# The first four chunks by halves, one stretch for Y, D and G, and a new order

## The chip, the core and the metric

The kernel runs on one core of a Trainium2 chip. The core has TensorE (PE, matmuls; its weight loads are listed as PEld), VectorE (DVE), ScalarE (ACT), GpSimd (POOL) and the DMA queues, of which this kernel uses those of SyncE (SP) and ScalarE. The metric is device time in microseconds. The kernel before takes 120.8 us (median of 3 runs, 120.77 to 120.96).

## The reference

Two parts run one after the other. The first is a Mamba-2 style scan over 4 sequences of 768 positions with 8 heads, in chunks; the second is a feed-forward layer with GELU.

```python
# first part, per sequence and head, chunk after chunk
cum   = cumsum(log(clip(a, 1e-6, 1)))
M     = (C @ B.T) * exp(cum_i - cum_j) * (i >= j)
y     = M @ x + (C @ state) * exp(cum_i)
state = exp(cum_last) * state + sum_j exp(cum_last - cum_j) * outer(B_j, x_j)
# second part, on all 3072 tokens of 256 values
h   = y_tokens @ w_in               # 256 -> 2048
out = gelu_tanh(h) @ w_out          # 2048 -> 256
```

The result does not depend on the chunk length; the kernel uses chunks of 128 positions instead of 32.

## The kernel before

A sequence has 6 chunks of 128, so there are 24 chunks, worked in 12 pairs u = 0 to 11. Instead of exp and log the kernel takes products of the clipped decays, by a scan that runs backwards through a chunk (lines 325 to 329). B is multiplied by these products and C by their reciprocals, so that the Gram product of both already holds the decay.

Each pair goes through these steps. G is the Gram matmul of scaled B and C (line 574, tiles of 32x128). M masks it with a triangle (line 584). D makes each chunk's addition to the state (line 607, tiles of 128x32), S updates the state and SP spreads it into blocks (lines 655 and 662). Y is the output of the scan, from the state (line 629) and from M (line 638), both in tiles of 128x32; yev moves it from PSUM to SBUF. Then s1 is the first feed-forward matmul in eight steps of four (line 688), gelu takes each of them on ACT (line 692), and s2 is the second feed-forward matmul: for each of the two chunks four groups of four (line 706), then oev copies the result out and store writes it.

Sequence 0 is prepared in its own way, because nothing can start before it. Its first four chunks (pairs 0 and 1) come with four loads aq.0 to aq.3 of the decays, one for each chunk of all sequences, one load each of B and C (load_bc0, line 147) and one of x (load_x4, line 180). With four consecutive positions in a partition, chunk 0 is in partitions 0 to 31, chunk 1 in 32 to 63, and so on. clipq, Rq (the scan), tpq (a transpose) and recip0 make the factors; mulb and mulc (lines 413 and 406) scale B and C; mulc keeps even and odd heads apart, with zeros between. tw transposes them on TensorE (line 422) and ew copies the result to SBUF. x4 casts x, XX brings it into the right order and XD makes D for pairs 0 and 1 (lines 542 and 552). The mask of pair 0 is split: M.0.0 on DVE, and GE (ACT) with ME (POOL, line 595) for the rest. Chunks 4 and 5 come with bc1 and mul1, T1, ce1, bh1, N1, bn1. The other sequences come with one load each of B and C, with mul, T, E, F, N and bn.

The weights are loaded in four quarters each (load_wi, load_wo) and cast in halves (wi.q.k, wo.q.k). The first s1 of a pair needs the cast quarter 0 of w_in and yev of the pair.

The order of all work is written out by hand in the string ORDERED. Each engine takes its steps from it in that order and in no other; an ending such as :A, :D or :P says which engine runs a step that can run on several. The loads and stores stand in SP's queue in the same order (or ACT's, with :A). `~n` puts n units of filler on TensorE, matmuls with zeros of 128 columns a unit (line 676); `name+n` puts them in front of an s1 step.

PSUM is narrow: two banks "hp" are shared by s1, D, XX, tw and pp, one bank "o" by s2 and some of the first transposes, two pairs "ga" and "gb" by G and transposes, and one bank "yb" by Y and the last s2.

Of the kernel before, what the change touches and what calls it, by code (L numbers as in the profile page):

```python
# [29 lines left out]
mul.1.0 s1.1.7 load_x.3 Y.2 yev.2.0.2 s2.0.1.1.o wo.2.1:D T.1.1 wo.2.0:D gelu.1.7 s1.2.0 gelu.2.0  # L30
castx.3.None load_x.4 T.1.0 s1.2.1 E.1.0 load_bc.2.1 s2.0.0.2.o E.1.1:A s1.2.2 gelu.2.1 N.1 F.1
castx.4.None gelu.2.2 bn.1:D wo.3.1:D load_bc.2.0 s2.0.1.2.o load_x.5 s1.2.3 wo.3.0:A G.3 M.3.0
s1.2.4 load_bc.3.1 gelu.2.3 load_x.6 s1.2.5 gelu.2.4 s2.0.0.3.o gelu.2.5 s1.2.6 s2.0.1.3.o
gelu.2.6 load_x.7 M.3.1 s1.2.7 D.3 oev.1 S.3.0 oev.0 G.4 gelu.2.7 SP.6 S.3.1 s2.1.0.0.o D.4
castx.7.None Y.3 s2.1.0.1.o s2.1.0.2.o yev.3.0.2 s2.1.0.3.o s1.3.0 S.4.0 M.4.0 S.4.1 M.4.1 mul.2.1
oev.2 s1.3.1 mul.2.0 gelu.3.0 s2.1.1.0.o s2.1.1.1.o gelu.3.1 s1.3.2 load_bc.3.0 s2.1.1.2.o
s2.1.1.3.o gelu.3.2 T.2.1 s1.3.3 SP.8 T.2.0 gelu.3.3 s1.3.4 oev.3:D load_x.8 castx.5.None:A E.2.0
s2.2.0.0.o SP.9 s2.2.0.1.o gelu.3.4 s1.3.5 N.2 s1.3.6 bn.2 E.2.1 s2.2.0.2.o SP.7 gelu.3.5 gelu.3.6
s2.2.0.3.o Y.4 castx.6.None:D yev.4.0.2 D.5 oev.4:D G.5 S.5.0 store.2 s1.3.7 s1.4.0 gelu.3.7
gelu.4.0 s2.2.1.0.o s1.4.1 gelu.4.1 s2.2.1.1.o M.5.0 SP.10 s2.2.1.2.o s1.4.2 s2.2.1.3.o s1.4.3  # L40
gelu.4.2 s1.4.4 M.5.1 gelu.4.3 F.2 G.6 oev.5:D D.6 S.6.0 Y.5 gelu.4.4 S.6.1 D.7 S.7.0 s2.3.0.0.o
S.7.1 M.6.1 store.0 yev.5.0.2 s1.4.5 s2.3.0.1.o castx.8.None:D s1.4.6 load_x.9 store.1 gelu.4.5
SP.14 SP.12 store.3 gelu.4.6 s1.4.7 gelu.4.7 s2.3.0.2.o s1.5.0 gelu.5.0 s2.3.0.3.o M.6.0 oev.6
s1.5.1 s1.5.2 gelu.5.1 s2.3.1.0.o load_x.10 G.7 D.8 castx.10.None S.8.0 SP.15 castx.9.None:D SP.13
Y.6 gelu.5.2 mul.3.1 s1.5.3 s1.5.4 gelu.5.3 gelu.5.4 s2.3.1.1.o s2.3.1.2.o s2.3.1.3.o oev.7 s1.5.5
gelu.5.5 mul.3.0 yev.6.0.2:D s1.5.6 s2.4.0.0.o gelu.5.6 s1.5.7 M.7.0 s2.4.0.1.o s2.4.0.2.o M.7.1
s1.6.0 s2.4.0.3.o T.3.0 gelu.5.7 s1.6.1 T.3.1 oev.8 s2.4.1.0.o store.6 gelu.6.0 gelu.6.1 store.4
s2.4.1.1.o s1.6.2 gelu.6.2 s1.6.3 store.5 s2.4.1.2.o s2.4.1.3.o E.3.0 s1.6.4 gelu.6.3 oev.9:D
E.3.1 gelu.6.4 s1.6.5 N.3 s2.5.0.0.o s1.6.6 bn.3 gelu.6.5 Y.7 F.3 G.8 s1.6.7 s2.5.0.1.o s2.5.0.2.o
s2.5.0.3.o yev.7.0.2:D gelu.6.6 gelu.6.7 oev.10:D s1.7.0 s1.7.1 gelu.7.0 SP.16 s2.5.1.0.o  # L50
s2.5.1.1.o s2.5.1.2.o M.8.1 M.8.0 gelu.7.1 s1.7.2 s2.5.1.3.o s1.7.3 G.9 gelu.7.2 Y.8 gelu.7.3
oev.11 store.9 M.9.1 D.9 load_x.11 S.9.0 s1.7.4 S.9.1 M.9.0 s2.6.0.0.o gelu.7.4 s2.6.0.1.o
s2.6.0.2.o s2.6.0.3.o oev.12:D s1.7.5 SP.18 s1.7.6 yev.8.0.2:D s2.6.1.0.o gelu.7.5 G.10 D.10 Y.9
# [32 lines left out]
def kernel(  # L86
# [92 lines left out]
    def load_x4():  # L179
        nc.sync.dma_start(out=x4_t, in_=x[0, :, 0:R4 * Q, :].rearrange("h (p r) d -> p h (r d)", r=R4))  # L180
# [599 lines left out]
    for i in (1, 2, 0):  # L780
# [153 lines left out]
```

## Time and profile before

| | before |
|---|---|
| median of 3 runs | 120.8 us (120.77 to 120.96) |
| profiled execution | 121.85 us |
| its span, first to last instruction | 120.1 us |
| mean granted TensorE clock | 0.971 |
| TensorE busy | 113.1 us, 94% |
| DVE, ACT, POOL busy | 74.5, 73.0, 16.2 us |
| start of G.0, Y.0, s1.0.0 | 9.25, 12.85, 14.92 us |
| one s1 step or s2 group of 4 matmuls at full clock | 0.437 us |

Busy times are shares of one profiled execution. In the row of slices each digit is a fortieth of the span, in tenths; PEclk is the clock that TensorE was granted. A wait names the engine or transfer that came last. A busy TensorE is not one at its peak: at half clock the same matmuls look just as busy and take twice as long.

### The profile page before, as it was taken

Reading aid. Unit: us, or ns where it says so; the run is one execution under the profiler, and the core shown is the slowest. Engines: PE = TensorE matmul, PEld = TensorE weight load, DVE = VectorE, ACT = ScalarE, POOL = GpSimd, SP = SyncE. Lnnn points to the kernel's source line nnn. Section 1 sums busy time; section 2 is a strip of 40 time slices with the busy share of each in tenths; the row PEclk is TensorE's granted clock in tenths of the full one; section 3 lists DMA queues with packets and bytes.
Section 4 is the critical chain, followed back from the end, with each engine's and each line's share of the span. In section 5 each row is a group of like instructions: output and inputs, shape, how many; then the busy total and the mean of one; then the engine's idle time right before and its main releaser. Section 6 shows DMA issues by size and latency. Waiting matters only on the chain.

```text
span 120.1 us, 3430 instructions
## 1 busy us (share of the span) xinstructions
PE 113.1 (94%) x1456; PEld 94.1 (78%) x1456; DVE 74.5 (62%) x147; ACT 73.0 (61%) x142; POOL 16.2 (14%) x33
## 2 busy tenths in 40 slices
PE   6948999999999999999999999999999999999990
PEld 2324457888887998989799979888989899999970
DVE  6289799999979977969597356798645003102000
ACT  2227649966974658668665574543786565576430
POOL 7315776205300020020000000000000000000000
PEclk9997559999999999999999999999999999999999
DMA  3999989996949877900400060006100001001521
GB/s 70 223 294 278 371 216 270 359 247 102 271 76 215 174 136 159 196 8 0 132 5 0 0 124 13 5 6 212 49 27 17 0 5 44 0 5 46 175 87 44
DMA packets 37662, 14.00 MB, mean 117 GB/s; under 512 B 31824, under 2 KB 36112, under 8 KB 37648
## 3 DMA queue, kind: packets, MB, share of 16 engines
q1 hardware_dynamic: 37456, 13.70, 44.5%
q8 instruction: 11, 0.18, 0.6%
q10 hardware_dynamic: 192, 0.10, 0.4%
q14 instruction: 3, 0.02, 0.1%
HBM read 10.65 MB, written 3.15 MB: 115 GB/s over the span
## 4 chain that ended last, share of the span: by engine, by line
PE 87%; DMA 7%; ACT 2%; DVE 1%; issue 0%; ACTq 0%
PE hp L688 36%; PE o_ps L706 32%; DMA a_t<-in_a_dram 5%; PE ga L574 3%; PE yb L706 3%; PE yb L629 3%; PE yb L638 2%; DMA aq_t<-in_a_dram 2%; ACT gT L692 1%; PE yb L676 1%; PE hp L607 1%; PE ga L500 1%; PE gb L481 1%; PE ga L481 1%; PE hp L542 1%; DVE bh L315 1%
## 5 line engine op out<-in xcount | busy, mean ns | idle before, releaser
L692 ACT ACTIVATE gT<-hp 128x512 bf16<-128x512 f32 x96 | 54.2, 597 | 28.0 <-PE hp L688 27.6
L688 PE MATMUL hp<-xm,w_in_sb 128*128 128x256 bf16 x384 | 54.7, 277 | 0.2 <-ACT gT L692 0.2
L706 PE MATMUL o_ps<-w_out_sb,gT 128*128 128x256 bf16 x352 | 47.4, 273 | 0.0
L688 PEld LDWEIGHTS <-w_in_sb 128*128 128x128 bf16 x384 | 41.1, 114 | 3.7 <-issue 1.7
L706 PEld LDWEIGHTS <-gT 128*128 128x128 bf16 x384 | 37.1, 98 | 4.1 <-issue 0.2
L315 DVE COPY o_sb<-o_ps 128x256 f32<-128x256 f32 x9 | 3.8, 425 | 20.5 <-PE o_ps L706 20.3
L584 DVE TENSOR_TENSOR m<-ga,tri 128x1024 bf16<-128x1024 f32 x12 | 14.6, 1217 | 0.7 <-PE gb L574 0.6
L584 DVE TENSOR_TENSOR m<-gb,tri 128x1024 bf16<-128x1024 f32 x11 | 13.4, 1220 | 0.9 <-PE gb L574 0.9
L313 POOL CAST x<-x_t 128x512 bf16<-128x512 f32 x5 | 4.5, 893 | 27.4 <-DMA x_t<-in_x_dram 27.4
L662 DVE SCALAR_TENSOR_TENSOR sp_new<-s_new,pend,bmask 128x256 bf16<-128x256 f32 x17 | 8.0, 473 | 0.0
L676 PE MATMUL yb<-wz 128*128 128x512 bf16 (+2 forms) x20 | 6.8, 489 | 1.1 <-DVE warm L219 1.1
L311 ACT ACTIVATE o_sb<-o_ps 128x256 f32<-128x256 f32 x13 | 4.8, 381 | 4.7 <-PE o_ps L706 4.7
L638 PE MATMUL yb<-m,x 128*32 128x128 bf16 x192 | 6.4, 226 | 0.0
L655 DVE SCALAR_TENSOR_TENSOR s_new<-s_new,pend,hp 128x64 f32<-128x64 f32 x13 | 3.6, 279 | 4.5 <-PE hp L607 4.1
L311 ACT ACTIVATE xm<-yb 128x512 bf16<-128x512 f32 x7 | 4.2, 598 | 2.4 <-PE yb L638 2.0
L676 PEld LDWEIGHTS <-wz 128*128 128x128 bf16 x20 | 2.2, 119 | 4.2 <-issue 2.4
L629 PE MATMUL yb<-ce,sp_new 128*32 128x128 bf16 x160 | 5.4, 225 | 0.0
L574 PE MATMUL ga<-ce,bh 32*128 32x256 bf16 x48 | 4.9, 283 | 0.3 <-ACT ce L311 0.3
L574 PE MATMUL gb<-ce,bh 32*128 32x256 bf16 x48 | 4.9, 284 | 0.0
L638 PEld LDWEIGHTS <-x 128*32 128x32 bf16 x192 | 3.9, 100 | 0.7 <-ACT x L311 0.7
L706 PE MATMUL yb<-w_out_sb,gT 128*128 128x256 bf16 x32 | 4.5, 273 | 0.0
L315 DVE COPY bh<-ga 128x768 bf16<-128x768 bf16 (+1 forms) x4 | 3.3, 824 | 1.5 <-PE ga L481 1.3
(110 smaller groups left out, 87.7 us busy)
## 6 DMA issues: line engine op xcount, KB each, us to landing
out_dram<-o_sb SPq DMA_DIRECT2D x24, 128.0 KB, 1.8
x_t<-in_x_dram SPq DMA_DIRECT2D x20, 128.0 KB, 4.1
wf<-in_moe_w_in_dram SPq DMA_DIRECT2D x4, 512.0 KB, 7.2
wf<-in_moe_w_out_dram SPq DMA_DIRECT2D x4, 512.0 KB, 7.0
bc_t<-in_C_dram SPq DMA_DIRECT2D x3, 384.0 KB, 4.1
bc_t<-in_B_dram SPq DMA_DIRECT2D x3, 384.0 KB, 6.0
x_t<-in_x_dram SPq DMA_DIRECT2D x1, 512.0 KB, 6.2
bcf<-in_C_dram SPq DMA_DIRECT2D x1, 256.0 KB, 3.2
```

Of the source, the lines that this page charges most:

```text
L311: nc.scalar.activation(o, i, AF.Copy)
L313: nc.gpsimd.tensor_copy(out=o, in_=i)
L315: nc.vector.tensor_copy(out=o, in_=i)
L574: nc.tensor.matmul(out=gbank(g)[:, 256 * k:256 * k + 256], lhsT=bh_of(2 * u + k)[gs], rhs=ce_of(2 * u + k)[gs], start=True, stop=True, til ...
L584: nc.vector.tensor_tensor(out=m_of(u)[:, 2 * i:2 * i + 2].rearrange("p g k e t -> p (g k e) t"), in0=gx[i].rearrange("p g (k t) -> p (g k) ...
L629: nc.tensor.matmul(out=y4[32 * j:32 * j + 32, k, w], lhsT=sp[:, 32 * h:32 * h + 32], rhs=ce_of(gc)[:, h % 2], start=first(j), stop=False, ...
L638: nc.tensor.matmul(out=y4[32 * j:32 * j + 32, k, w], lhsT=X16[u][:, k, 32 * h:32 * h + 32], rhs=m[:, h // 2, h % 2, :], start=first(j), st ...
L662: nc.vector.scalar_tensor_tensor(out=sp_new.rearrange("p (g d) -> p g d", g=4), in0=(XN[0][:, H * D:H * D + 64] if gc == 0 else state[("s" ...
L676: nc.tensor.matmul(out=t[:, 0:m * 128], lhsT=wz, rhs=w3.to_broadcast([128, m, 128]), start=True, stop=True, skip_group_check=True)
L688: nc.tensor.matmul(out=hp[:, j * T:(j + 1) * T], lhsT=w_in_k[:, w, q, k], rhs=xm[:, w, u * T:(u + 1) * T], start=(w == 0), stop=(w == 1))
L692: nc.scalar.activation(gts[u][:, 2 * i:2 * i + 2], hps.pop((u, i)).rearrange("p (j t) -> p j t", j=2), AF.Gelu_apprx_tanh)
L706: nc.tensor.matmul(out=ops[gc], lhsT=gts[u][:, fi, k * Q:(k + 1) * Q], rhs=w_out_sb[:, fi, :], start=(fi == 0 and (u > 0 or k == 0)), stop ...
```

## The change

Four things change.

The work on the first four chunks is done in two halves, of chunks 0 and 1 and of chunks 2 and 3, that is partitions 0 to 63 and 64 to 127. Loads of B, C and x, clip, scan, transpose, reciprocal, the three scalings, the transposes on TensorE and the casts of x become two steps each with the same row length. An eviction ew already covered two chunks; its size stays. The loads of B and C may stand in ACT's queue. Pair 0 then needs only the first half and pair 1 only the second.

From pair 3 to pair 10, Y of a pair, D of the next and G of the next are one step, that runs without another TensorE step between them.

The whole order is written anew. At the start mulb.0, mulc.0.0, mulb.1 and mulc.1.1 go to POOL, all four x4 casts to ACT. load_wo.0 stands between load_wi.1 and load_wi.2, and bc1, x.2 and the loads for sequence 1 stand behind the weights. The second feed-forward matmul of pair 0 begins after s1.0.3 instead of after s1.1.2. Casts wo.0.0, wo.0.1, wo.1.0, wo.3.0 and wi.3.0 are on ACT. The filler changes: 60, 4, 2 and 11 units before, 46, 8, 5, 1, 4 and 12 after, with 6 in front of s1.0.0 and 4 in front of s1.2.0.

```diff
-load_bc0.1 c_wz load_aq.0 c_ident c_zero c_cz load_aq.1 load_aq.2:S c_unp load_bc0.0 load_aq.3
-c_m4 c_sel clipq c_tri Rq tpq recip0 mulb mulc.0 load_x4 mulc.1 c_warm load_a.0 ~60 tw.0 tw.1
-load_a.1:A peq ew.0.0:A load_wi.0 c_bmask tw.2 clip ew.0.1:A load_bc1.1 ew.0.2:A ew.1.2:A
-load_wi.1 ~4 G.0 ew.1.0 x4.1 ew.1.1 GE.3 ~2 ppq x4.0:P c_par XX.0 R M.0.0 ME.3 pendq GE.2 XD.0
-ME.2 xn.0 SP.0 xn.1 wi.0.1:A ~11 Y.0 c_m8 S.0.0 tp2 wi.0.0 S.0.1 XX.1 recip1 XD.1 yev.0.0.2
-wi.1.1:A S.1.0 s1.0.0 wi.1.0 load_wi.2 xn.2 wi.2.0 mul1.1 SP.1 gelu.0.0 load_wi.3 G.1 s1.0.1
...
+load_bc0.1.0 c_wz c_ident load_aq.0 load_aq.1 c_zero load_bc0.0.0 c_cz c_sel load_a.1:A c_unp
+load_x4.0 load_bc0.1.1:A clipq.0 load_aq.2 load_aq.3:S Rq.0 load_bc0.0.1:A load_x4.1 load_wi.0
+c_warm c_tri tpq.0 recip0.0 mulb.0:P mulc.1.0 load_wi.1 clipq.1 load_wo.0 x4.1.0 Rq.1 ~46 tw.0.0
+mulc.0.0:P tw.2.0 c_m4 ~8 tw.1.0 ew.1.0 peq c_bmask load_wi.2 ew.2.0:A ew.0.0:A ~5 G.0 tpq.1
+load_a.0:A x4.0.0 ~1 ppq GE.3 pendq mulb.1:P GE.2 ~4 XX.0 recip0.1 XD.0 load_wi.3 mulc.1.1:P M.0.0
+x4.1.1 S.0.0 SP.0 xn.0:D load_bc1.1 tw.2.1 load_bc1.0 ~12 tw.0.1 xn.1 load_wo.1 S.0.1 mulc.0.1
+ew.2.1:A ME.3 x4.0.1 load_wo.2 ME.2 clip Y.0 ew.0.1:A wi.0.0:A load_wo.3 tw.1.1 yev.0.0.2 XX.1
+ew.1.1 XD.1 wi.0.1 S.1.0 s1.0.0+6 xn.3 wi.1.1 wo.0.1:A wi.1.0 xn.2:D wi.2.1 S.1.1 gelu.0.0 s1.0.1
+G.1 SP.1 gelu.0.1 R s1.0.2 wo.0.0:A gelu.0.2 wi.2.0 M.1.1 M.1.0 s1.0.3 s2.0.0.0.o s1.0.4 load_x.2
+load_bc.1.1 gelu.0.3 gelu.0.4 s1.0.5 s2.0.1.0.o wi.3.0:A c_m8 SP.2 tp2 wi.3.1 Y.1 gelu.0.5 mul1.0
+yev.1.0.2 s1.0.6 tp6.2 recip1 gelu.0.6 s1.0.7 gelu.0.7 T1.0 wo.1.1 mul1.1 s1.1.0 wo.2.0 bh1 tp6.0
+wo.1.0:A T1.1 s1.1.1 tp6.3 N1 load_bc.1.0 gelu.1.0 s2.0.0.1.o pe wo.2.1 gelu.1.1 pp s2.0.1.1.o
+c_par ce1.1 bn1:D ce1.0 wo.3.1 s1.1.2 gelu.1.2 pend:D s1.1.3 SP.3 gelu.1.3 G.2 wo.3.0:A s2.0.0.2.o
...
-    def f_tw(i):
+    def f_tw(i, w):
         t = psh.tile([128, 512], FP32, name="hp") if i else pso.tile([128, 512], FP32, name="o_ps")
-        T0[("w", i)] = t.bitcast(BF16)[:, 0:R4 * 128]
+        T0[("w", i, w)] = t.bitcast(BF16)[:, 0:T]
         for r in range(R4):
-            src = cz[:, i - 1, r] if i else bc0s[0][:, 0, r]
-            nc.tensor.transpose(out=T0[("w", i)][:, r * 128:(r + 1) * 128],
-                                in_=src.rearrange("p h n -> p (h n)"), identity=ident)
+            src = cz[half(w), i - 1, r] if i else bc0s[0][half(w), 0, r]
+            nc.tensor.transpose(out=T0[("w", i, w)][:, r * 64:(r + 1) * 64],
+                                in_=src.rearrange("p h n -> p (h n)"), identity=ident[half(w), half(w)])
...
+    for u in range(3, NU - 1):
+        y = steps[f"Y.{u}"]
+        gone = [steps.pop(f"D.{u + 1}"), steps.pop(f"G.{u + 1}")]
+        y.fn = lambda fs=(y.fn, gone[0].fn, gone[1].fn): [f() for f in fs]
...
```

## The prediction

> **What bounds the kernel now.** I read the engine table and the 40 slices first, then windows of the start, then the timeline of the first 30 us, then the waits of TensorE. The profiled execution took 121.85 us (span 120.1 and 1.75 around it), 0.9% above the median of the three runs, 120.8. I sum in its own time and carry the difference over to the median unchanged. A change under 0.2% (0.24 us) can't be told from none.
>
> ```profile
> PE 113.1 (94%) x1456; PEld 94.1 (78%) x1456; DVE 74.5 (62%) x147; ACT 73.0 (61%) x142; POOL 16.2 (14%) x33
> PE   6948999999999999999999999999999999999990
> PEclk9997559999999999999999999999999999999999
> DMA  3999989996949877900400060006100001001521
> ```
>
> TensorE is full from the fourth slice on. After 15 us its list of waits has only this:
>
> ```profile
> PE hp L688 <- ACT gT L692: 0.2, 1, 0.2
> ```
>
> So the end is the moment at which dense work starts plus the work left over, and only three things can move it: an earlier s1.0.0 (first matmul of the feed-forward part), less time on TensorE afterwards, or more useful work put into its weak stretches. Where those are, the windows tell (columns: length, busy of PE, PEld, DVE, ACT, POOL, granted clock, DMA share, GB/s):
>
> ```profile
> 7.31:10.72 3.41, 2.46 (x30) 1.55 (x32) 3.03 (x10) 2.48 (x8) 0.78 (x2) 1.00 1.04 258
> 10.72:14.13 3.41, 3.41 (x73) 1.58 (x69) 3.30 (x10) 2.09 (x6) 2.92 (x7) 0.50 1.03 361
> 14.13:17.54 3.41, 3.41 (x56) 1.65 (x53) 2.38 (x5) 1.72 (x5) 2.61 (x4) 0.50 1.08 275
> 40.00:60.00 20.00, 20.00 (x302) 17.70 (x300) 16.03 (x31) 13.37 (x25) 1.23 (x2) 1.00 0.52 114
> ```
>
> From 10.8 to 17.5 us the clock is 0.50: a "full" TensorE does half. The start itself (start, duration, engine, line):
>
> ```profile
> 5.50 0.23 DVE L325 TENSOR_SCALAR acq<-aq_t 128x128 f32<-128x128 f32 x1 [2.36 <-DMA aq_t<-in_a_dram]
> 6.22 0.40 DVE L339 STREAM_TRANSPOSE rt<-rq_t 128x128 f32<-128x128 f32 x1
> 6.96 0.69 DVE L413 TENSOR_TENSOR bc0s<-bcf,rt 128x512 bf16<-128x512 f32 x1
> 7.57 0.76 DVE L406 TENSOR_TENSOR cz<-bcf,pt 128x256 bf16<-128x256 f32 x2
> 9.25 0.28 PE L574 MATMUL ga<-ce,bh 32*128 32x256 bf16 x2 [0.26 <-ACT ce L311]
> 10.55 1.57 POOL L595 TENSOR_SCALAR_AFFINE_SELECT m<-ge 128x512 bf16<-128x512 bf16 x2 [1.32 <-ACT ge L589]
> 11.57 1.35 PE L676 MATMUL yb<-wz 128*128 128x512 bf16 x3
> 12.85 0.40 PE L638 MATMUL yb<-m,x 128*32 128x128 bf16 x8
> 14.92 1.05 PE L688 MATMUL hp<-xm,w_in_sb 128*128 128x256 bf16 x4
> 16.01 0.60 ACT L692 ACTIVATE gT<-hp 128x512 bf16<-128x512 f32 x1 [0.21 <-PE hp L688]
> 28.46 2.01 POOL L313 CAST x<-x_t 128x512 bf16<-128x512 f32 x1 [6.57 <-DMA x_t<-in_x_dram]
> ```
>
> The chain is decays landed (5.5), scaled B and C, G.0 (9.25), masks, Y.0 (12.85), s1.0.0 (14.99 on the chain of waits), first GELU (16.01).
>
> **Part 1: one stretch for Y, D and G.** A change between full-array and tiled matmuls costs about 0.10 us on each side. The timeline shows it at Y.2: eight s1 matmuls from 26.92 need 0.87 (27.79), Y begins 27.89, its 32 matmuls need 0.45, the next step begins 28.45. Counting mode changes from s1.0.0 to the end in both orders gives 39 and 39: the old order already ran most of these steps side by side (Y.4 D.5 G.5; G.6 D.6 Y.5 D.7). Value 0; bounds one stretch either way, 0.2 us.
>
> **Part 2: the halves, up to G.0.** A half is 64 partitions of the same row length, and I take the duration to go by row length (a 64x384 clip takes 0.53, the 128x128 one 0.23). So halves double the count: clip, scan, turn, reciprocal, mulb, two mulc are 0.23+0.42+0.40+0.35+0.69+0.84 = 2.9 us more, plus two x4 casts (0.63 each). What pays is that the first half starts when two of the four aq loads are there. They hold the same first places on ACT's queue, whose second issue ends near 1.9 and lands 2.9 after its start of 1.4: 4.3 instead of 5.50. Then 1.16 for clip, scan and turn (5.50 to 6.66 before): 5.45. On SP the halves of C, B and x4 go out as four transfers of 128 to 256 KB with aq.3, ahead of w_in; C.1, B.1 and a.1 take ACT's queue, 0.46 each, until about 3.7, delaying ACT's table load to 5.0, while its first x4 cast waits for data until about then. wi.0 is behind 1.65 MB instead of 1.70 and lands near 10.0 as before; wo.0 comes before wi.2, and the bc1, x.2 and bc.1 loads move behind w_out, about 5 us later than before but still ahead of their users (mul.1.1 ran at 27.51, data there at 21.9).
>
> mulb and one mulc of each half are now POOL's, in a row: mulb.0, mulc.0.0, mulb.1, mulc.1.1, then the masks ME.3 and ME.2. No row shows a POOL multiply. Low bound: DVE's 0.69 and 0.42. High bound: the POOL cast of 512 that took 2.01 beside DVE's multiplies, against 0.61 alone. I take the ratio of the lone casts, 0.61 to DVE's 0.42 = 1.45, because it is the same shape: 1.0 and 0.6, four together 3.2 us. So mulb.0 ends 6.45, mulc.0.0 7.05, transposes 7.3, eviction 0.40: G.0 at 7.8, 1.45 earlier.
>
> The Trainium skill (GPSIMD Engine Reference, section 4.1 Engine selection) says that two-input elementwise work there is about twice as slow as on VectorE. By it the four would be 4.4 us, and the sum below would come out near 121.5.
>
> **From G.0 to s1.0.0.** tpq.1 stands on DVE behind ew.1.0 and peq: done 8.4. mulb.1 to 9.4, mulc.1.1 to 10.0, ME.3 and ME.2 1.57 more: 11.6. TensorE's queue waits at tw.2.1 for mulc.1.1, and behind it stand 12 units of filler, tw.0.1 and Y.0; with the clock dropping at 10.8 as before they end 11.35, hidden by the masks. Y.0 11.6 (was 12.85), 0.83 long: 12.45. Then in series tw.1.1 0.25, XX.1 and XD.1 1.31 (13.68 to 14.99 before), and six filler units that s1.0.0 now carries, 0.70 at the rate of the eleven (1.28): **s1.0.0 at 14.7, 0.3 earlier**. Of 1.25 gained at Y.0, 0.95 goes to steps queued before s1.0.0. ACT's list (three x4 casts, two GE, xn.1, three evictions, wi.0.0, yev.0) ends at about 13.65, inside that.
>
> **From s1.0.0 to s1.2.0.** GELU of pair 0 runs 16.01 to 22.67 before gelu.1.0 begins, ACT working 6.05 of 6.66. The new order puts three weight casts and bh1 among them and takes xn.3, pend and ce1.1 away: eight GELUs 4.4 + 0.65 + 0.63 + 0.60 + 0.38 + 0.65 = 7.3, plus the same idle 0.6. From 15.7 that is 23.6, 0.9 late. To yev.2: 3.85 + 0.94 + 0.65 + 0.60 + 0.3 idle; s1.2.0 at 29.95 instead of 29.23, 0.7 late. But TensorE has used the wait: eight s2 groups of pair 0 are done by then instead of four, 4 x 0.437 = 1.75, less T.1.1 (0.34) not yet done. Ahead by 1.4 - 0.7 = **0.7 us**. The four fillers before s1.2.0 lie in ACT's time; if ACT is early they cost 0.21.
>
> After that the same work is left. Tail: the last eviction moves from ACT (0.38) to DVE (0.43); stores 19 and 21 are issued between 22 and 23 but done before the last eviction. 0 to 0.1.
>
> Sum: 121.85 - 0.7 = 121.15, against the median **120.1 us**.
>
> **The rivals.**
> POOL is the bound, slower. Place: tw.2.1, behind which Y.0 and s1.0.0 queue. Every microsecond on the four multiplies moves s1.0.0 by about 1.2, as the filler then runs wholly at half clock. The lead of 0.7 is gone when they take 3.8 instead of 3.2. At 4.4: mulc.1.1 11.25, fillers and transposes 13.05, s1.0.0 16.15, lead -0.75: 121.5. For it: the 2.01 us cast, which shows POOL held up while DVE multiplies, as DVE does here (mulc.1.0, scan). Against: every other lone POOL cast stays at 0.61.
> No net change: ACT idles 0.5 to 0.9 more between GELUs than before. For: ACT becomes the longest list from 15 to 30. Against: DVE's list there (M.1 after G.1) fits. 120.8.
> The clock stays full. More early work in TensorE could keep it from dropping at 10.8; then Y.0, XX.1, XD.1 and the filler save about 1.0, the first s1 steps 0.4 more: 118.7. Against: the filler before 10.8 is about what it was.
> The clock stays half one stretch of 3.4 longer, to 21: half of 3.4, some 0.6 of it hidden by ACT: +1.1 to 1.7, 121.5.
> As to that stretch, the trace keeps 0.50 through 10.72:14.13 although TensorE is busy all of it. The Trainium skill (TensorE: Matmul & The Clock Gate, Part 1) says one busy window of about 3.4 us suffices for full rate; by that rule the release comes at 14.1, the lead grows to about 1.5, and the time is 119.3; the trace of before speaks against it.
>
> **How the numbers follow.** Forecast 0.33 (119.8 to 120.5), full or earlier clock 0.17, no change 0.10, POOL 0.30, longer half clock 0.10. Faster 0.50, same 0.10, slower 0.40. Leaving out the far half of the full clock and some of the worst of the last two gives 118.8 to 121.6.
>
> **What would show it.** G.0 near 7.8, Y.0 near 11.6, s1.0.0 near 14.7; POOL's TENSOR_TENSOR near 1.0 and 0.6; clock 0.50 from 10.8 to 17.5; first GELU of pair 2 near 30; no TensorE waits after it. Wrong if POOL's four multiplies take 3.8 or more, if the clock changes its stretch, or if Y.3 or a later stretch waits for M or SP.

## The result and the profile after

The changed kernel takes 125.69 us (median of 4 runs, 125.28 to 126.66), the kernel before 120.78 beside it (120.70 to 120.96). The ratio is 1.042, 95% interval 1.035 to 1.048: slower by 4.9 us, where 0.7 less was forecast and the range ended at 121.6. To read what follows, one thing must be known: the profiled execution of before had half the clock for 6.8 us (mean granted clock 0.971), and of 62 later runs of that kernel only 3 show a mean as low (0.972), the other 59 0.995 or more, all 62 with a median of 120.5 us.

From the page of the changed kernel, the engines, TensorE's slices, its clock and the DMA share:

```profile
PE 115.4 (93%) x1472; PEld 95.2 (77%) x1472; DVE 73.8 (60%) x147; ACT 76.7 (62%) x146; POOL 19.4 (16%) x38
PE   6747999999999999999999999999999999999980
PEclk9997555999999999999999999999999999999999
DMA  2999988889994569932200600014110020112022
```

The list of TensorE's waits after 15 us is empty now. The windows of its start (length, busy of PE, PEld, DVE, ACT, POOL, granted clock, DMA share, GB/s):

```profile
7.31:10.72 3.41, 2.29 (x27) 1.13 (x26) 2.51 (x8) 1.88 (x6) 1.71 (x5) 1.00 1.05 285
10.72:14.13 3.41, 2.79 (x60) 1.16 (x58) 3.31 (x7) 2.50 (x6) 3.34 (x6) 0.55 1.00 369
14.13:17.54 3.41, 3.41 (x73) 1.99 (x66) 1.46 (x5) 2.31 (x5) 2.55 (x7) 0.50 0.92 237
17.54:20.95 3.41, 3.41 (x23) 1.93 (x21) 3.08 (x4) 2.25 (x4) 0.89 (x3) 0.50 0.84 281
40.00:60.00 20.00, 20.00 (x297) 17.76 (x296) 15.58 (x26) 14.11 (x27) 1.38 (x2) 1.00 0.57 120
```

The clock is 0.50 from about 11.0 to 21.3 us, 3.4 longer than in the profile of before. The steady part (40 to 60 us) looks the same. The start from the timeline (start, duration, engine, line, in brackets the wait before it):

```profile
3.81 0.22 DVE L329 TENSOR_SCALAR acq<-aq_t 64x128 f32<-64x128 f32 x1 [0.73 <-DMA aq_t<-in_a_dram]
5.71 1.05 POOL L417 TENSOR_TENSOR bc0s<-bcf,rt 64x512 bf16<-64x512 f32 x1 [2.94 <-DMA bcf<-in_B_dram]
6.72 0.62 POOL L410 TENSOR_TENSOR cz<-bcf,pt 64x256 bf16<-64x256 f32 x1
8.07 0.22 DVE L329 TENSOR_SCALAR acq<-aq_t 64x128 f32<-64x128 f32 x1 [2.27 <-DMA aq_t<-in_a_dram]
9.48 0.28 PE L577 MATMUL ga<-ce,bh 32*128 32x256 bf16 x2 [1.12 <-DVE ce L319]
10.19 1.05 POOL L417 TENSOR_TENSOR bc0s<-bcf,rt 64x512 bf16<-64x512 f32 x1 [1.55 <-DVE rt L343]
11.20 0.63 POOL L410 TENSOR_TENSOR cz<-bcf,pt 64x256 bf16<-64x256 f32 x1
11.91 1.23 POOL L598 TENSOR_SCALAR_AFFINE_SELECT m<-ge 128x512 bf16<-128x512 bf16 x2
12.21 1.46 PE L679 MATMUL yb<-wz 128*128 128x512 bf16 x3
13.93 0.41 PE L641 MATMUL yb<-m,x 128*32 128x128 bf16 x8
16.94 1.27 PE L691 MATMUL hp<-xm,w_in_sb 128*128 128x256 bf16 x5
```

The first half starts early (3.81 against 5.50), as it should. The second half's clip then waits 2.27 us for its decays, G.0 stands behind it by way of the eviction ew.1.0 in VectorE's queue and comes at 9.48, Y.0 at 13.93 and s1.0.0 at 16.94. Between G.0 and Y.0 a second thing shows: tw.2.1 waits for mulc.1.1 (the multiply at 11.20, done 11.83), and the 12 units of filler behind it run at half clock from 12.21 to 13.67, past the end of the masks at 13.14. They stand on the chain of waits with 1.40 us. On SyncE's queue there is a gap just there (columns as above):

```profile
2.26 0.63 SPq L184 DMA_DIRECT2D x_t<-in_x_dram  x1
3.90 0.37 SPq L160 DMA_DIRECT2D aq_t<-in_a_dram  x1
```

aq.3 is ready to go at 2.89 and goes at 3.90. The chain of waits gives the reason: its first two pieces are C's load, 0.81 to 3.89, and aq_t from 3.90 for 4.14 us. So the issue waited for an earlier load to land; what in the queue makes it wait is not shown.

### The profile page after: what moved, and what is told of

Its sections match the earlier page's. It is cut to its first block, busy times and chain, and to the rows that moved or that the text cites. A ratio compares the mean times of both kernels' runs of the same rounds, so it can differ in the third digit from the quotient of the medians.

```text
span 123.5 us, 3488 instructions
## 1 busy us (share of the span) xinstructions
PE 115.4 (93%) x1472; PEld 95.2 (77%) x1472; DVE 73.8 (60%) x147; ACT 76.7 (62%) x146; POOL 19.4 (16%) x38
## 4 chain that ended last, share of the span: by engine, by line
PE 85%; DMA 6%; ACT 2%; DVE 2%; issue 1%; POOL 1%; POOLq 0%
PE hp L691 36%; PE o_ps L709 31%; DMA aq_t<-in_a_dram 3%; PE ga L577 3%; PE yb L709 3%; PE yb L641 3%; PE yb L632 3%; DMA bcf<-in_C_dram 2%; ACT gT L695 1%; PE yb L679 1%; PE ga L503 1%; PE gb L484 1%; PE ga L484 1%; PE hp L679 1%; PE hp L545 1%
## 5 line engine op out<-in xcount | busy, mean ns | idle before, releaser
L695 ACT ACTIVATE gT<-hp 128x512 bf16<-128x512 f32 x96 | 54.8, 597 | 26.9 <-PE hp L691 26.8
L709 PE MATMUL o_ps<-w_out_sb,gT 128*128 128x256 bf16 x352 | 48.4, 273 | 0.0
L691 PEld LDWEIGHTS <-w_in_sb 128*128 128x128 bf16 x384 | 41.6, 115 | 4.2 <-issue 2.4
L319 DVE COPY o_sb<-o_ps 128x256 f32<-128x256 f32 x11 | 4.7, 424 | 26.5 <-PE o_ps L709 24.5
L679 PE MATMUL yb<-wz 128*128 128x512 bf16 (+2 forms) x21 | 7.3, 484 | 1.1 <-DVE warm L223 1.1
L315 ACT ACTIVATE xm<-yb 128x512 bf16<-128x512 f32 x11 | 6.6, 596 | 2.1 <-PE hp L610 1.5
L315 ACT ACTIVATE o_sb<-o_ps 128x256 f32<-128x256 f32 x11 | 4.2, 382 | 2.7 <-PE o_ps L709 2.7
L632 PEld LDWEIGHTS <-sp_new 128*32 128x32 bf16 x160 | 3.0, 98 | 1.8 <-issue 1.2
```

Source lines behind the costliest of these rows:

```text
L315: nc.scalar.activation(o, i, AF.Copy)
L319: nc.vector.tensor_copy(out=o, in_=i)
L632: nc.tensor.matmul(out=y4[32 * j:32 * j + 32, k, w], lhsT=sp[:, 32 * h:32 * h + 32], rhs=ce_of(gc)[:, h % 2], start=first(j), stop=False, ...
L679: nc.tensor.matmul(out=t[:, 0:m * 128], lhsT=wz, rhs=w3.to_broadcast([128, m, 128]), start=True, stop=True, skip_group_check=True)
L691: nc.tensor.matmul(out=hp[:, j * T:(j + 1) * T], lhsT=w_in_k[:, w, q, k], rhs=xm[:, w, u * T:(u + 1) * T], start=(w == 0), stop=(w == 1))
L695: nc.scalar.activation(gts[u][:, 2 * i:2 * i + 2], hps.pop((u, i)).rearrange("p (j t) -> p j t", j=2), AF.Gelu_apprx_tanh)
```

## The experiments

Each ratio below is to the kernel before, run beside (medians 120.5 to 120.6), with its 95% interval.

**What the landmarks say together.** One execution each; the last columns are TensorE's last matmul less s1.0.0, what comes after it, and the span. "Start of before" is run e8 below.

| | G.0 | Y.0 | s1.0.0 | to last matmul | after it | span |
|---|---|---|---|---|---|---|
| before, more filler (e4) | 9.39 | 11.78 | 13.71 | 101.8 | 3.2 | 118.8 |
| start of before, changed order behind it (e8) | 9.08 | 11.95 | 13.89 | 101.5 | 3.2 | 118.6 |
| changed, more filler (e3) | 9.41 | 12.76 | 14.84 | 102.8 | 3.5 | 121.2 |
| changed | 9.48 | 13.93 | 16.94 | 103.0 | 3.5 | 123.5 |

The first three ran at full clock. The 4.8 us between the last row and e8 are 2.3 of clock (last against third row, 2.1 of it before s1.0.0) and 2.5 that stay at full clock: 0.95 at s1.0.0, 1.3 behind it, 0.3 in the tail. The 2.3 take in the 12 filler units that e3 moved away as well, for which its expectation puts 0.3. These are single executions: by the medians of the runs the same two parts are 1.8 and 3.6, since e3's runs spread over 2.2 us and its profiled one took 122.98.

### The clock

e3, the changed kernel with more filler:

```diff
-... Rq.1 ~46 tw.0.0 ... ~5 G.0 ... tw.2.1 load_bc1.0 ~12 tw.0.1
+... Rq.1 ~76 tw.0.0 ... ~24 G.0 ... ~12 tw.2.1 load_bc1.0 tw.0.1
```

> The changed kernel with filler put into three holes of TensorE in which it waits anyway: 76 units instead of 46 before tw.0.0, 24 instead of 5 before G.0, and the 12 units behind tw.2.1 moved ahead of it. Theory C (the clock falls at 10.9 us because TensorE was too idle from 5.3 to 11, and that is most of the loss): the clock stays 1.00 past 14 us or is half for 7 us at most, and the time falls by 1.5 to 3 us to 122.7 to 124.2. Theory L: clock 0.50 for 10 us as before, time 125.2 to 125.7 (the moved filler gives 0.3).

Measured: 123.87 (122.19 to 124.43), ratio 1.033 (1.027 to 1.039), clock 0.997 in the profiled run. The clock, with the moved filler in it, is worth 1.8 us by the medians and 2.3 by the profiled executions; the 3.4 us that are left against the kernel before (123.87 against 120.5) are something else.

e4, the same for the kernel before (`~60` to `~92`):

> The kernel before with 92 units of filler instead of 60 ahead of tw.0, which ends the filler at about 7.6 us, when tw.0 could begin, instead of 5.9. If the clock's fall at 10.8 us comes of the idle 1.9 us: clock 1.00 through 14 us and time 119.3 to 120.3. If the work from 7.7 to 10.7 decides, nothing changes: 120.6 to 121.0.

Measured: 120.88, ratio 1.004 (1.001 to 1.007), clock 0.995 to 1.0. No gain, because that kernel has its full clock nearly always.

e7, the kernel before with the changed kernel's first count of filler (`~60` to `~46`):

> The kernel before with 46 units of filler at the start instead of 60, as the changed kernel has, and nothing else. Theory C (the filler ahead of G.0 is what keeps the clock up): granted clock 0.95 to 0.975, time 122.0 to 123.0. Rival (the clock of the changed kernel falls for the gaps of its own start and not for the 14 units): clock 0.995 or more, time 120.3 to 120.8.

Measured: 122.49 (122.30 to 122.54), ratio 1.015 (1.009 to 1.021); clock 0.958 in the profiled run. (One run of the four lists 0.995 and took as long, 122.52; it has no trace, and its mean clock does not show the time before the clock first comes up, as is told below. The reading rests on the trace, where against e4 s1.0.0 comes 1.3 us later, at 14.97, and the last matmul 0.5 us later still.) Fourteen units of filler, matmuls with zeros, decide 1.9 us.

e15, the changed kernel with `~46` to `~60`:

> The changed kernel with 60 units of filler at the start instead of 46 and nothing else. Theory C14 (the 14 units decide, as they did in the kernel before): granted clock 0.99 or more, time 123.6 to 124.3. Rival (the changed start has further gaps, the one of 1.1 us ahead of G.0 above all, that drop the clock as well): clock 0.95 to 0.97, time 125.2 to 126.2.

Measured: 125.36 (125.03 to 125.58), ratio 1.038 (1.032 to 1.043), clock 0.959 to 0.972. The units alone do not repair the changed kernel, so the rival holds: its start has further gaps on TensorE, in e15 one of 1.12 us ahead of G.0 and two of 0.7. Which of them counts was not tried by itself. The rows of the clock on the pages of e3, e7 and e15, one fence each (e4's is the same as e3's):

```profile
PEclk9999999999999999999999999999999999999998
```
```profile
PEclk9995557999999999999999999999999999999999
```
```profile
PEclk9998555999999999999999999999999999999999
```

A window of the start goes with it. From 3.80 to 10.60 us TensorE worked this much in the changed kernel (first fence) and in e7 (second):

```profile
3.80:10.60 6.80, 4.12 (x38) 1.88 (x38) 4.19 (x13) 3.90 (x9) 3.19 (x6) 1.00 1.11 250
```
```profile
3.80:10.60 6.80, 4.99 (x34) 2.38 (x34) 5.01 (x14) 2.61 (x9) 1.08 (x3) 0.90 1.00 255
```

Over all 18 profiled kernels of this study, those with 5.11 us or less in that window lost the clock between 9 and 12.3 us (seven of them: before 4.40, changed 4.12, e1 4.66, e5 4.85, e7 4.99, e15 4.98, e16 5.11). Of the eleven with 5.27 or more only e9 lost it (6.69 here), at 14.4 and right after a wait of 1.5 us. The border between 5.11 and 5.27 was found afterwards in these same executions; no run tested it, and e9 shows that it is not the whole rule. The half clock lasted 6.8 us or 10.2 (in e16 in two pieces).

These rows and the mean clock hide one thing: they begin where the clock first comes up, and until then the filler runs at half speed. When that happens differs from execution to execution. The same 60 units in the profiled execution of before (first fence) and in e2 (second):

```profile
1.06 4.80 PE L676 MATMUL yb<-wz 128*128 128x512 bf16 x15 [1.06 <-DVE warm L219]
```
```profile
1.05 6.28 PE L625 MATMUL yb<-wz 128*128 128x512 bf16 x15 [1.05 <-DVE warm L168]
```

In before the filler's weight loads start 0.43 us apart up to about 3.9 us and 0.21 apart from then on; in e2 they stay 0.43 apart to the last one at 6.57. So in before TensorE is done early and idles for 1.85 us ahead of tw.0, at 7.71, which e2's filler nearly reaches: its window from 3.80 to 10.60 is fuller, and its clock never falls. The first rise lies between 3.9 us (before) and 7.0 (e8) in the traces, and where the clock falls it falls 3.41 us after that rise (e7), 6.83 (six kernels) or 10.24 (e9). That the rare stretch of the kernel before comes of an early rise is read from these executions and was not tried apart.

### The order behind s1.0.0 and the stretch

e2, the kernel before with the stretches: the loop of the diff that joins Y, D and G, and the tokens D.4 to D.11 and G.4 to G.11 taken out of the order.

> The kernel before with one part of the change alone: from pair 3 to 10, Y, the next D and the next G are one step; S, M and SP that used D or G ahead of Y follow it, all else stands as it was. Prediction's count (39 mode changes in both): 120.6 to 121.0, the same as before. Rival S (the stretch itself makes TensorE wait, since D and G now come with the masks of Y): 0.5 us or more slower, with waits of TensorE on DVE at Y or on M.

Measured: 121.49, ratio 1.008 (1.005 to 1.012), clock 0.997. TensorE waits that were not there (from its list of waits):

```profile
PE yb L587 <- DVE xm L264: 0.4, 1, 0.4
PE o_ps L655 <- ACT o_sb L260: 0.2, 1, 0.2
```

So rival S holds: the stretch forced on an order made for something else costs 1.0 us (121.49 against 120.49), of which these two waits are 0.6.

e8, the order of before up to s1.0.0 and the changed order with its stretches from there on:

```diff
 load_bc0.1 c_wz load_aq.0 ... XD.1 yev.0.0.2 wi.1.1:A S.1.0        (as before)
-s1.0.0 wi.1.0 load_wi.2 ...                                        (rest of before)
+load_wo.0 load_wi.2 load_wi.3 load_bc1.0 load_wo.1 load_wo.2 load_wo.3
+s1.0.0 xn.3 wi.1.1 wo.0.1:A ... oev.23:D store.23                  (rest of the changed order)
```

> The order of before up to s1.0.0, with its whole loads and its filler, and from there on the changed order with the stretches (four units of filler before s1.2.0 kept, six before s1.0.0 not). Theory R (about 1.2 us of the loss lie between s1.0.0 and the fourth pair and 0.3 in the tail): s1.0.0 at 13.7, clock 0.995 or more, time 121.5 to 122.1. Rival S (all of the loss that is not clock lies in the start): 120.3 to 120.9.

Measured: 120.29 (119.95 to 121.09), ratio 0.997 (0.993 to 1.000), clock 1.0. The theory that 1.5 us lie in the new order falls: with the old start it is as good as the old order, and what is lost apart from the clock lies in the start and in what the start leaves for later. In the steady part both are alike: the passes of Y, D and G for pairs 4 to 11, added up from the starts of the matmuls in the trace, take 8.5 us in e4 and 8.5 in e3.

e12, e8 without the four units before s1.2.0 (`s1.2.0+4` to `s1.2.0`), for a kernel faster than both:

> The kernel with the start of before and the changed order from s1.0.0 on (120.29, ratio 0.9967), without the four units of filler before s1.2.0, which took 0.41 us there less the 0.11 of a usual step. Theory F (TensorE is the bound there): 0.3 us less, 120.0, ratio 0.994 to the kernel before. Rival (the GELU chain is the bound there, and the filler lay in its time): no difference, 120.3.

Measured: 120.29 (120.04 to 120.88), ratio 0.998 (0.996 to 1.000). No difference to e8, and neither is told apart from the kernel before with certainty.

### The loads

e1, the changed kernel with the decays of the second half issued first:

```diff
-... load_aq.0 load_aq.1 c_zero ... load_a.1:A ... clipq.0 load_aq.2 load_aq.3:S Rq.0 load_bc0.0.1:A
+... load_aq.0 load_aq.1 load_aq.2 load_aq.3:S c_zero ... clipq.0 Rq.0 load_a.1:A load_bc0.0.1:A
```

> The changed kernel with one edit: the two loads of decays for the second half (aq.2, aq.3) are issued right behind aq.0 and aq.1, and a.1 goes behind C.1. Theory L (the late second half holds up DVE, which stands at clipq.1 until 8.04 us with the eviction for G.0 behind it): clipq.1 near 6.2, G.0 near 8.2 instead of 9.48, s1.0.0 1 to 1.5 us earlier than 17.1, time 124.0 to 124.8 against 125.7. Theory C (the loss is the half clock until 21 us, and the early work is thin whatever it waits for): G.0 earlier, but clock 0.50 for 10 us again and the time within 0.5 us of 125.7.

Measured: 125.93 (125.35 to 126.16), ratio 1.046 (1.040 to 1.051). The second clip moves from 8.07 to 5.66, but the second half of B is late in its place (timeline). G.0 comes at 9.15 and s1.0.0 at 17.52, and the clock is 0.50 for 10 us again. The late multiply:

```profile
10.78 1.05 POOL L417 TENSOR_TENSOR bc0s<-bcf,rt 64x512 bf16<-64x512 f32 x1 [2.37 <-DMA bcf<-in_B_dram]
```

e5, the kernel before with only its loads of C, B and x cut in halves:

```diff
-load_bc0.1 ... load_bc0.0 load_aq.3 ... load_x4
+load_bc0.1.0 load_bc0.1.1 ... load_bc0.0.0 load_bc0.0.1 load_aq.3 ... load_x4.0 load_x4.1
```

> The kernel before with only its loads of C, B and x for the first four chunks cut in two of 64 partitions each, all work on them whole as before. Theory T (smaller transfers are slower and use up more completion counters, which is why the halves brought nothing; in the filler run the 128 KB halves of C and B on ACT's queue took 5.1 us from issue to landing, in the kernel before with more filler the whole 256 KB loads 3.0 and 4.0): C, B or x arrive at least 0.7 us later, G.0 at 10.0 or later instead of 9.4, time 121.0 to 122.0. Rival N (two halves cost what the whole does, the late start has another cause): G.0 within 0.3 of 9.4, time 120.2 to 120.8.

Measured: 122.89 (122.55 to 123.43), ratio 1.020 (1.012 to 1.028), clock 0.958 to 0.972. G.0 stays at 9.40, so that step of the expectation missed; what is late is behind it. B makes mulb wait. Each half's issue takes 0.6 to 0.7 us on SyncE's queue, where a whole load takes 0.43, so the load of the other decays goes out at 5.58 instead of 3.28 (e4) and makes their clip and all behind it on VectorE late:

```profile
7.12 0.69 DVE L413 TENSOR_TENSOR bc0s<-bcf,rt 128x512 bf16<-128x512 f32 x1 [0.76 <-DMA bcf<-in_B_dram]
9.51 0.72 DVE L325 TENSOR_SCALAR ac<-a_t 64x384 f32<-64x384 f32 x1 [0.83 <-DMA a_t<-in_a_dram]
12.07 1.19 DVE L584 TENSOR_TENSOR m<-ga,tri 128x1024 bf16<-128x1024 f32 x1
```

M.0.0 is at 12.07 (10.53 in e4), Y.0 at 13.31. The clock falls too, at 12.3 us, after M.0.0 has begun, so the 1.5 us up to there belong to the loads and not to the clock; how the rest parts, this run does not show. Nor does any run show that halves use up more completion counters, which the expectation gives as a cause.

e6, e3 with the loads of C, B and x whole again (`load_bc0.1.0`, `load_bc0.0.0`, `load_x4.0` stand for the whole load, their second halves go):

> The changed kernel with more filler (full clock, 123.87) with its loads of C, B and x made whole again at the places of their first halves on SyncE's queue; the work on them stays in halves. Theory T: the second half no longer waits for its B and x, aq.3 lands earlier, G.0 at 9.0 or earlier instead of 9.4, Y.0 at 12.2 or earlier instead of 12.76, time 122.8 to 123.4. Rival N (the decays' last two loads and GpSimd's multiplies set the start, not the halves): G.0 9.4, s1.0.0 within 0.3 of 14.84, time 123.6 to 124.2.

Measured: 123.57 (123.07 to 124.18), ratio 1.024 (1.017 to 1.031). The second clip starts at 7.76 and G.0, behind 24 units of filler, at 9.97. The whole loads bring 0.3 us at most, which is within the scatter of the runs.

e10, e6 with aq.2 and aq.3 issued behind aq.1 and `~24 G.0` to `~10 G.0`:

> The kernel with whole loads and more filler (123.57) with aq.2 and aq.3 issued right behind aq.1, a.1 behind them, and 10 units of filler ahead of G.0 instead of 24, which stood in front of G.0 there (it began at 9.97). Theory L (the second half's decays, and nothing behind them, hold the start): second clip by 6.0, G.0 at 9.3 or earlier, s1.0.0 at 14.3 or earlier instead of 15.36, time 122.4 to 123.0. Theory T (the transfers as a whole set the start; what one load gains another loses): s1.0.0 14.6 or later, time 123.2 or more.

Measured: 123.49 (123.34 to 124.44), ratio 1.027 (1.023 to 1.030). The second clip is at 6.38, s1.0.0 at 15.11, and nothing is waiting for decays, but the turn of the second half stands behind the eviction ew.1.0 on VectorE, and that waits for TensorE:

```profile
6.38 0.23 DVE L329 TENSOR_SCALAR acq<-aq_t 64x128 f32<-64x128 f32 x1
9.16 0.42 DVE L319 COPY ce<-hp 128x256 bf16<-128x256 bf16 x1 [1.90 <-PE hp L426]
9.84 0.40 DVE L343 STREAM_TRANSPOSE rt<-rq_t 64x128 f32<-64x128 f32 x1
10.39 1.05 POOL L417 TENSOR_TENSOR bc0s<-bcf,rt 64x512 bf16<-64x512 f32 x1 [0.61 <-DVE rt L343]
```

So the loads are one limit among several near each other; taking them away uncovers a queue.

### VectorE and GpSimd

e13, e10 with the second half's turn, reciprocal and multiplies right behind its scan and the first half's multiplies:

```diff
-... mulb.0:P mulc.1.0 ... Rq.1 ~76 tw.0.0 mulc.0.0:P ... G.0 tpq.1 ... mulb.1:P ... recip0.1 ... mulc.1.1:P
+... mulb.0:P mulc.0.0:P mulc.1.0 ... Rq.1 tpq.1 recip0.1 mulb.1:P mulc.1.1:P ~80 tw.0.0 ... G.0 ...
```

> The kernel with whole loads and early decays (123.49) in which the turn of the second half no longer stands behind the eviction ew.1.0 on VectorE, nor its multiplies behind the mask bmask on GpSimd: tpq.1 and recip0.1 right behind Rq.1, mulb.1 and mulc.1.1 right behind mulc.0.0; 80 units of filler in place of 76. Theory Q (once data is early, the place in VectorE's and GpSimd's queues is what holds the second half): mulb.1 starts by 9.0 instead of 10.39, Y.0 at 12.3 or earlier instead of 13.0, s1.0.0 by 14.4 instead of 15.11, time 122.3 to 123.0. Rival (M.0.0 and the GpSimd masks set Y.0 whatever the second half does): Y.0 within 0.3 of 13.0, time 123.2 to 123.8.

Measured: 124.15 (123.16 to 124.35), ratio 1.028 (1.022 to 1.034). mulb.1 starts at 8.69, 1.7 earlier, and Y.0 only 0.14 earlier (12.86), since bmask and the masks of pair 0 now stand behind the multiplies on GpSimd:

```profile
8.69 1.05 POOL L417 TENSOR_TENSOR bc0s<-bcf,rt 64x512 bf16<-64x512 f32 x1 [0.86 <-DVE rt L343]
10.39 0.31 POOL L237 MEMSET bmask<- 128x256 bf16 x1
11.69 1.22 POOL L598 TENSOR_SCALAR_AFFINE_SELECT m<-ge 128x512 bf16<-128x512 bf16 x2
```

The rival is right that Y.0 hardly moves, whatever the order within GpSimd's list. The chain of waits goes from the two multiplies through bmask (done 11.75) to a step on VectorE and tw.0.1 at 12.64, so GpSimd's list sets Y.0 here through bmask and not through the masks of pair 0.

e9, e3 with `mulb.1:P` and `mulc.1.1:P` on VectorE (`:D`):

> The changed kernel with more filler (full clock, 123.87) with the two multiplies of the second half that GpSimd had, mulb.1 and mulc.1.1, on VectorE. Theory P (GpSimd's multiplies set the start, as the rival in the prediction had it): mulc.1.1 ends 0.5 us earlier than 11.76, s1.0.0 at 14.3 or earlier, time 123.4 or less. Theory V (VectorE's list is what is too long, because it stands idle for 2.3 us until the decays of the second half have landed): M.0.0 starts 1.0 us later than 10.4, Y.0 moves with it, s1.0.0 14.8 to 15.4, time 123.8 to 124.6.

Measured: 124.65 (124.07 to 125.31), ratio 1.035 (1.030 to 1.039). M.0.0 starts at 11.54 instead of 10.41 and Y.0 at 13.89 instead of 12.76; a part of the 0.8 us is clock (0.972 in the profiled run), so s1.0.0, at 16.93, can't be used. VectorE has no room for them either.

e14, the kernel before with `mulb mulc.0` on GpSimd, full height:

> The kernel before with mulb and mulc.0 on GpSimd instead of VectorE, at full height of 128 partitions. It measures the disputed price alone. Theory P (GpSimd 1.05 and 0.62 as at half height, beside mulc.1 on VectorE): both done by 8.1, G.0 within 0.4 of the usual 9.1 to 9.4, time 120.2 to 120.9. Rival (two-input work is twice VectorE's, or the height counts there): 1.3 us or more for mulb, G.0 9.8 or later, time 121.0 or more.

Measured: 121.34 (120.96 to 123.83), ratio 1.008 (1.004 to 1.012). The price of mulb was right and the time was not: mulb takes 1.05 at 128 partitions as at 64. mulc.0 takes 0.81 and not 0.62, but it takes 0.80 at half height in e6 too, again beside mulc.1 on VectorE, so a multiply goes by its row length. And mulc.1 beside it on VectorE takes 0.94 instead of 0.42:

```profile
6.52 1.05 POOL L413 TENSOR_TENSOR bc0s<-bcf,rt 128x512 bf16<-128x512 f32 x1 [3.75 <-DVE rt L339]
7.53 0.81 POOL L406 TENSOR_TENSOR cz<-bcf,pt 128x256 bf16<-128x256 f32 x1
6.91 0.94 DVE L406 TENSOR_TENSOR cz<-bcf,pt 128x256 bf16<-128x256 f32 x1
```

M.0.0 is 0.4 later (10.94 against 10.53 in e4), and s1.0.0 14.12 instead of 13.71.

e11, e3 with a.0 loaded behind a.1, and clip and the scan R in VectorE's idle stretch ahead of the second half's clip:

```diff
-load_a.1:A ... mulc.1.0 load_wi.1 clipq.1 ... ME.2 clip Y.0 ... gelu.0.1 R s1.0.2
+load_a.1:A load_a.0:A ... mulc.1.0 load_wi.1 clip R clipq.1 ... ME.2 Y.0 ... gelu.0.1 s1.0.2
```

> The changed kernel with more filler (123.87) with a.0 loaded right behind a.1, and clip and the scan R of the other sequences in the stretch of 2.3 us in which VectorE waits for the second half's decays, instead of behind Y.0 and s1.0.1. Theory V (VectorE's list: R behind s1.0.1 makes M.1 late for Y.1, which lost 0.51 there, and mul1 late for T1, which lost 0.92, against the kernel with the start of before): the two losses go, s1.0.0 to the end 101.5 to 101.9 instead of 102.8, time 122.6 to 123.1. Rival (the load of a.0 so early delays the loads behind it by as much): B or x of the first half 0.5 us or more later, time 123.6 to 124.6.

Measured: 123.69 (123.30 to 124.26), ratio 1.028 (1.025 to 1.032). Behind s1.0.0 the theory holds in part: Y.1 takes 0.77 us as in e8 (1.28 in e3) and T1.1 0.71 (1.14 in e3, 0.22 in e8), and s1.0.0 to the last matmul falls from 102.8 to 102.1. Ahead of it the second clip waits for VectorE until 9.03 and s1.0.0 comes at 15.85, 1.0 later. What is gained behind is paid in front.

e16, the kernel before in its own order, loads whole, all multiplies on VectorE, only the work in halves:

```diff
-... clipq c_tri Rq tpq recip0 mulb mulc.0 load_x4 mulc.1 ... ~60 tw.0 tw.1 ... tw.2 ... G.0 ew.1.0 x4.1 ew.1.1
+... clipq.0 c_tri Rq.0 tpq.0 recip0.0 mulb.0 mulc.0.0 load_x4 mulc.1.0 c_warm clipq.1 Rq.1 tpq.1 recip0.1 mulb.1
+mulc.0.1 mulc.1.1 ... ~60 tw.0.0 tw.1.0 ... tw.2.0 ... G.0 tw.0.1 tw.1.1 tw.2.1 ew.0.1 ew.2.1:A x4.1.0 x4.1.1 ew.1.1
```

> The kernel before in its own order, loads whole and all multiplies on VectorE, with only the work on the first four chunks in halves, the second half's steps right behind the first's (no stretches). Theory H (a half costs what the whole does, so halving adds 2.9 us to VectorE ahead of M.0.0): steps of 64 partitions last what those of 128 did, M.0.0 starts 2 us or more later than 10.5, Y.0 13.5 or later, time 122.5 to 125.0 (the upper part if the clock falls). Rival (the first half's lead of about 1 us on the way to G.0 pays for it): G.0 8.5 or earlier, time 120.0 to 121.5.

Measured: 126.78 (125.72 to 128.27), ratio 1.047 (1.039 to 1.055). The timeline shows both sides of the idea:

```profile
4.26 0.22 DVE L329 TENSOR_SCALAR acq<-aq_t 64x128 f32<-64x128 f32 x1 [1.12 <-DMA aq_t<-in_a_dram]
7.32 0.23 DVE L329 TENSOR_SCALAR acq<-aq_t 64x128 f32<-64x128 f32 x1
8.10 0.28 PE L577 MATMUL ga<-ce,bh 32*128 32x256 bf16 x2
12.61 1.19 DVE L587 TENSOR_TENSOR m<-ga,tri 128x1024 bf16<-128x1024 f32 x1
16.73 4.57 DVE L435 TENSOR_TENSOR bc0s<-bcf,pt 128x256 bf16<-128x256 f32 x1
```

G.0 comes 1.3 us earlier than in e4 (8.10 against 9.39). Its mask comes 2.1 later (12.61 against 10.53), because the second half's steps, as long as the whole ones were, stand between them; s1.0.0 is at 16.35. This is the share of the halves: the count doubles on whichever engine has them. The time of this run holds more than that, a clock of 0.957 and the multiply of 4.57 us in the last row, which the last section takes up.

## Why the prediction was wrong

**The frame.** The sum was made in an execution with half a clock from 10.8 to 17.5 and carried over to the median as if the median had it too. Its time of 121.85 stood 0.9% above the median, and that difference was the hint: 59 of 62 runs have a mean clock of 0.995 or more, and in the traces at full clock with that start (e2, e4, e8) s1.0.0 lies at 13.7 to 13.9, not at 14.92. The forecast of 14.7 was thus 0.9 later than usual and not 0.3 earlier. The frame is not the whole miss: in it the sum gave 121.15, and the profiled execution took 125.28, 4.1 more, 2.2 of it at s1.0.0 (16.94 against 14.7).

**The clock of the changed kernel.** The step "with the clock dropping at 10.8 as before they end 11.35, hidden by the masks" failed: the 12 units of filler ran at half clock from 12.21 to 13.67, the masks had ended at 13.14, and Y.0 came at 13.93, not 11.6. The step took the stretch of before as given; the rival of a stretch to 21 had a chance of 0.10 and a price of 1.1 to 1.7. It came, from 11.0 to 21.3; against full clock it costs 1.8 to 2.3, moved filler included (e3). That was readable in part: "the filler before 10.8 is about what it was" holds by the count, 64 units against 66 ahead of the first half-clock work, but not by the place, 46 in place of 60 at the start, and that place decides 1.9 us in e7. The other rival, full clock at 118.7, is refuted by e3: at full clock the changed kernel takes 123.87. By the Trainium skill (TensorE: Matmul & The Clock Gate, Part 1) one busy window of about 3.4 us is enough for full rate and an idle one drops it; the window's length agrees with stretches of 6.8 and 10.2, the rest does not: the clock fell with TensorE at work for 4.1 to 5.1 of 6.8 us, and in the changed kernel 14.13 to 17.54 was busy throughout and was followed by another 3.4 us at 0.50.

**Decays in time.** The step "tpq.1 stands on DVE behind ew.1.0 and peq: done 8.4" failed one place ahead: ew.1.0 itself stands behind clipq.1 and Rq.1, and they waited 2.27 us for aq.2 and aq.3, so that tpq.1 was done at 10.05. The working took aq.3 as going out with the halves of C, B and x; it goes out at 3.90, when C has landed. The forecast of 4.3 for the first half (3.81) and the claim that this half needs only two of four loads held. G.0 was to be at 7.8 and was at 9.48. e1, e6 and e10 add that this was one wait of several: with the decays early, B or VectorE's queue came next, and the gain was 0.4 us at most (123.49 against 123.87), within the scatter of the runs. A smaller term was short as well: the issues on ACT's queue, put at 0.46 each, took 0.56 to 0.69.

**GpSimd.** Its price, disputed in the forecast, was right: 1.05 and 0.62 us against 1.0 and 0.6, all four 3.35 against 3.2. The rule of twice VectorE's time (the Trainium skill, GPSIMD Engine Reference, section 4.1) would have been, as an estimate, 1.38 by VectorE's 0.69. The rival that GpSimd is the bound was right in its place and wrong in its price: mulc.1.1 ended at 11.83, not 10.0, because it started late, and e13 shows that an earlier start only moves the wait to bmask. e14 adds a term that the sum lacked, VectorE slowed beside it (0.94 instead of 0.42).

**Twice the work.** That halves double the count, 2.9 us, was in the text, and then paid by moving four multiplies. e16 shows it in full: G.0 1.3 earlier, its mask 2.1 later. In the changed order a part of the bill is the scan R behind s1.0.1: the forecast's "DVE's list there (M.1 after G.1) fits" did not ask what stands ahead of M.1 and T1. e3 against e8, the same order behind s1.0.0 but for R, one turn and one reciprocal, which e8 has ahead, loses 1.3 us there: 0.5 at Y.1 and 0.9 at T1, less small gains. In e3 the chain of waits goes through R there, and e11, with R moved ahead, wins half of it back. So the lead of 0.7 that TensorE should have had from earlier s2 groups is not there; with the old start it is 0.3 (101.5 in e8 against 101.8 in e4). It was sized in the profile of the half clock, where TensorE's waits for GELUs are another matter. The first GELU of pair 2 is at 34.4, where 30 was forecast.

**Part 1** was right for the changed order: 39 and 39 changes of mode, 8.5 and 8.5 us, no wait of TensorE after 36 us. The stretch alone in the old order costs 1.0 (e2). **The tail** of 0 to 0.1 is 0.3; e8 with the same tail has 0, so the order of the stores is not the cause. What is stays open, as does the exact share of loads, VectorE and GpSimd in the 0.95 us at s1.0.0 at full clock.

## What to carry to other kernels

Before a sum is made in a profiled execution, its clock and its distance to the median are to be compared: a rare execution taken for the usual one shifts every landmark. Halving work by partitions saves no engine time, since an instruction goes by its row length; it pays only where the engines have as much idle time as the second halves need, and here VectorE and GpSimd did not have it at the start (e16, e13). Filler on TensorE belongs to the change: add up its busy time in the 7 us ahead of the dense part before taking units or adding a wait there, and look at the filler's own durations, since the mean clock does not show when the clock first comes up. That the busy time of this window goes with the clock is read from 18 executions of nearly one kernel.

## What the hardware showed

Fourteen units of zeros, 46 instead of 60, cost 1.9 us in e7. A half of 64 partitions lasts what 128 do: 1.05 for GpSimd's multiply in e3 and e14, 0.42 for the scan of 128 columns in e4 and e3's first half. A load cut in half takes little less from issue to landing, and its issues take longer: on the same queue C and B of 256 KB took 3.0 and 4.0 us from issue to landing in e4 (first fence, the list of DMA issues), their halves of 128 KB 3.1 and 3.2 in e5, while the issue of C held SyncE's queue 0.43 us in e4 and its two halves 1.40 in e5 (second fence, from the timelines of e4 and e5):

```profile
bcf<-in_C_dram SPq DMA_DIRECT2D x1, 256.0 KB, 3.0
bcf<-in_B_dram SPq DMA_DIRECT2D x1, 256.0 KB, 4.0
```
```profile
0.81 0.43 SPq L147 DMA_DIRECT2D bcf<-in_C_dram  x1
0.81 1.40 SPq L147 DMA_DIRECT2D bcf<-in_C_dram  x2
```

The most striking is VectorE's multiply of 4.57 us in e16; the same step took 0.42 in e8 and 0.68 in the kernel before. It has two inputs in SBUF, begins at 16.73 and ends at 21.30, and GpSimd works through eleven casts from 14.84 on without a pause (its timeline in e16):

```profile
14.84 3.39 POOL L317 CAST w_in_sb<-wf 128x512 bf16<-128x512 f32 x6
18.18 1.17 POOL L317 CAST w_out_sb<-wf 128x512 bf16<-128x512 f32 x2
19.29 0.61 POOL L317 CAST x<-x_t 128x512 bf16<-128x512 f32 x1
19.85 1.17 POOL L317 CAST w_out_sb<-wf 128x512 bf16<-128x512 f32 x2
```

The last cast ends at 21.02 and the multiply right behind it. The Trainium skill (GPSIMD Engine Reference, section 1 Specifications) says that the two engines share their interfaces to SBUF and that VectorE's instructions with two SBUF inputs contend; the rows agree that a multiply beside GpSimd's work takes longer, as in e14. How long is another matter: the same step took 0.83 us in e14 at 14.28, amid six casts without a pause, and 0.45 in e7 at 15.34, amid four. So casts in a row alone do not hold VectorE, and what made it 4.57 in this one execution stays open.
